# Mean and scale rows of tiles 6, 7 and 8: fetched through DRAM instead of turned on the tensor engine

## The chip, the cores and the metric

The kernel runs on one core of one Trainium2 chip. The metric is the device time of one execution in microseconds (us); the profile of one such execution stands beside it. The engines are named as in the profile: PE (matmul; PEld is its weight load), DVE (vector), ACT (scalar), POOL (GpSimd) and SP, which here only issues DMAs, in the order of its queue.

## The reference

One block over x of 2048 rows by 576: a layer norm, a linear-attention branch with 32 heads of 18, and a gated feed-forward branch of width 4608, multiplied and added to x.

```python
xn = layernorm(x)                       # per row: (x - mean) / sqrt(var + 1e-5)
q, k, v = split_heads(xn @ wqkv)
phi = lambda t: where(t > 0, t + 1, exp(t)) + 1e-6
kv, z = sum over s of phi(k) v,  sum over s of phi(k)
o = phi(q) kv / (phi(q) z + 1e-6);   s = o @ wo
g = silu((gelu(xn @ w_gate) * (xn @ w_up)) @ w_down)
out = x + s * g
```

## The kernel before

The 2048 rows are 16 tiles of 128 rows (`n` or `t` 0 to 15), four to a block `tb` (0 to 3, `TT` = 4); two blocks make one half `s`. Everything here concerns the first 170 us, where x is normalized, k and v are projected and kv is summed. The order of each engine is the order in which the code records its instructions (`act` L123, `vec` L126, `mm` L129, `pool` L132, `dma` L135 pin them), so an instruction that waits holds up all that stands behind it on its engine.

Tiles 0 to 3 are normalized with rows on the partitions and then transposed on PE (`xt`). For tiles 4 to 15 x is loaded a second time already transposed (`xt[n]`, the part `D:` of a tile `x_n`; two tiles per load), so the mean and the scale are needed along the free axis:

- `spread(n0, n)` takes the statistics of n tiles on DVE (`bn`, `mv`) and their logarithm and exponent on ACT (`st`); `scales(n0)` makes the scale from them in three small DVE operations. Each gives one number per partition.
- `turn(n)` gets the rows on PE: it broadcasts mean and scale of one tile to 128 columns and transposes them into one PSUM bank, `ms` (two transposes, L233).
- The other way, in `scales` and `sort_rows`: one DVE copy puts the mean beside the scale, SP stores 128 x 4 numbers to DRAM (`md`) and reads them back broadcast over all partitions (`mx`, 128 x 512, 256 KB; it waits until `md` has landed), and ACT sorts them into four rows (`mr`, 128 x 512). Before the change this is done for pairs 8, 10, 12 and 14, and used for tiles 9 to 15; tile 8 is still turned.
- `place(n)` for n of 4 and more is `normalize`: DVE subtracts the mean (`x<-x,ms` or `x<-x,mr`, 128 x 768), multiplies with the scale twice (`xf_B`, 128 x 384), ACT makes the high words (`xo_B`) and DVE the low words. PE reads them for k, v and, once a block is complete, q.

`kv_tile(t)` is the pass over one tile: the products `kv_0`, then (even t) the pair sums `kv_a` of the two tiles before, the rows of tile t+1 (`sort_rows` if a pair stands ready in `mixed`, then `turn`), the post-processing of k on DVE, `kv_1`, `place(t+1)`, post-processing (`e_k`, `pk`, `va`), `kv_2`, and what the list `end` holds. `x_next(n)` takes the statistics of a pair when n is even. (For n of 4 and more an odd n leaves it without work.)

After tile 7 come the q products of blocks 0 and 1: `q_store(tb, gi)` is one product `q_gi` on PE, relu and exp on ACT (`e_q`), one DVE operation and one POOL addition (`ph`), and a store. The dictionary `behind` hangs other work after single ones: the statistics of pair 8 after (0, 0), `scales(8)` after (0, 1), the rows of tile 8 after (0, 3), `place(8)` after (1, 0), the statistics of pair 10 after (1, 1). Then tile 8 starts. The buffers `mx`, `mr` and `ph` share six slots (`gl_tile`).

Of the kernel before, what the change touches and what calls it, by code (L numbers as in the profile page):

```python
# [26 lines left out]
TT = TBN // P  # L27
# [64 lines left out]
def block_kernel(ctx, tc, x, xe, xt, wq_d, wkv_d, wo, wgu_d, wd_d, out):  # L92
# [6 lines left out]
    def bank(name):  # L99
        return ps.tile([P, 512], F32, tag="one", bufs=6, name=name)  # L100
# [13 lines left out]
    def gl_tile(shape, name, dt=F32):  # L114
        return sb.tile(shape, dt, tag="gl", bufs=6, name=name)
# [6 lines left out]
    def act(*args, **kw):  # L122
        pin(nc.scalar.activation(*args, **kw))  # L123

    def vec(op, *args, **kw):
        pin(getattr(nc.vector, op)(*args, **kw))  # L126
# [7 lines left out]
    def dma(out, in_, eng=None):  # L134
        tc.keep_in_program_order((eng or nc.sync).dma_start(out=out, in_=in_))  # L135
# [18 lines left out]
    def load_x(n, k):  # L154

        if n % 2 == 0:
            shape = [P, 2, 2, 3 * P] if n < TT else [P, 2, D + 6 * P]
            xstat[n // 2] = big(14 + n // 2 % 2, shape, F32, f"x_{n}")
        t = xstat[n // 2][:, n % 2 : n % 2 + k]
        if n == 0:  # L160
            for j in range(2):
                dma(out=t[:, 0, j], in_=xe[0:P, j], eng=(nc.sync, nc.scalar)[j])
        elif n < TT:
            dma(out=t, in_=xe[n * P : (n + k) * P].rearrange("(t p) j d -> p t j d", p=P))
        else:
            dma(out=t[:, :, 0:D], in_=x[n * P : (n + k) * P].rearrange("(t p) d -> p t d", p=P))
            dma(out=t[:, :, D:], in_=xt[n : n + k].rearrange("t p m -> p t m"))

    def spread(n0, n):

        bn = sb.tile([P, TT, 12], F32, tag="bn", bufs=2, name=f"bn_{n0}")
        mv = sb.tile([P, 2 * TT, 2], F32, tag="mv", bufs=4, name=f"mv_{n0}")
        for t in range(n):
            xs = xstat[(n0 + t) // 2][:, (n0 + t) % 2]
            for j in range(2):
                src = xs[:, j, 0:HALF] if n0 < TT else xs[:, j * HALF : (j + 1) * HALF]
                vec("bn_stats", out=bn[:, t, 6 * j : 6 * j + 6], in_=src)
            vec("bn_aggr", out=mv[:, t, :], in_=bn[:, t, :])
        st = sb.tile([P, 6, TT], F32, tag="st", bufs=4, name=f"st_{n0}")
        act(st[:, 0, 0:n], mv[:, 0:n, 1], AF.Ln, bias=eps_t)  # L180
        act(st[:, 2, 0:n], st[:, 0, 0:n], AF.Exp, scale=-0.5)
        vec("tensor_scalar", st[:, 1, 0:n], mv[:, 0:n, 1], LN_EPS, None, op0=ALU.add)
        mom[n0] = n, mv, st

    def scales(n0):

        n, mv, st = mom.pop(n0)
        v, r, c = (st[:, i, 0:n] for i in range(1, 4))
        if n == 1:
            vec("tensor_scalar", c, r, r, -0.5, op0=ALU.mult, op1=ALU.mult)  # L190
            vec("tensor_scalar", c, c, v, 1.5, op0=ALU.mult, op1=ALU.add)
            vec("tensor_scalar", c, c, r, None, op0=ALU.mult)
        else:
            vec("scalar_tensor_tensor", c, r, -0.5, r, op0=ALU.mult, op1=ALU.mult)
            vec("tensor_mul", c, c, v)
            vec("scalar_tensor_tensor", c, c, 1.5, r, op0=ALU.add, op1=ALU.mult)
        for t in range(n):
            scale_of[n0 + t] = mv[:, t, 0:1], c[:, t : t + 1]
        if n0 >= 2 * TT:
            vec("tensor_copy", st[:, 3, 2:4], mv[:, 0:2, 0])  # L200
            d = dr.tile([P, 4], F32, name=f"md_{n0}")
            mixed[n0] = g = gl_tile([P, P, 4], f"mx_{n0}")
            dma(out=d, in_=st[:, 3, :])
            dma(
                out=g.rearrange("p t c -> p (t c)"),
                in_=d.rearrange("t c -> (t c)")[None, :].to_broadcast([P, 4 * P]),
            )

    def sort_rows(n0):

        g = gl_tile([P, 4, P], f"mr_{n0}")
        act(g, mixed.pop(n0).rearrange("p t c -> p c t"), AF.Copy)
        for t in range(2):
            if n0 + t > 2 * TT:
                rows_of[n0 + t] = [g[:, None, i + t] for i in (2, 0)]

    def center(n):

        if n >= TT:
            return  # L220
        xs = xstat[n // 2][:, n % 2]
        m, r = scale_of.pop(n)
        vec("tensor_scalar", xs, xs, m, r, op0=ALU.subtract, op1=ALU.mult)

    def turn(n, new=bank):

        xs = xstat[n // 2][:, n % 2]
        if n in rows_of:
            return
        if n >= TT:  # L230
            xts[n] = t = bank(f"ms_{n}")
            for i, v in enumerate(scale_of.pop(n)):
                pin(nc.tensor.transpose(  # L233
                    t[:, i * P : (i + 1) * P], v.to_broadcast([P, P]), ident
                ))
            return
        tiles = [new(f"xt_{n}_{j}") for j in range(2)]
        xts[n] = [t[:, 0 : 3 * P].rearrange("p (k t) -> p k t", k=3) for t in tiles]
        for j in range(2):
            for k in range(3):  # L240
                pin(nc.tensor.transpose(xts[n][j][:, k, :], xs[:, j, k * P : (k + 1) * P], ident))  # L241
# [59 lines left out]
    mom, scale_of, xts, rows_of, mixed = {}, {}, {}, {}, {}  # L301
# [12 lines left out]
    def difference(s, i):  # L314
        f = xf[s]
        nm, a, b, o = SUMS[i]
        vec("tensor_sub", f[o], f[a], f[b])
        f[nm] = f[o]

    def keep(s, nm, o):  # L320
        d = dr.tile([P, 5, TBN], F32, name=f"kept_{s}_{nm}")
        dma(out=d, in_=o.bitcast(F32))
        store[s, nm] = d
# [59 lines left out]
    def load_q(j):  # L383
        raws["q", j] = big(12, [P, 2, 3, Q2], F32, f"rq_{j}")
        dma(out=raws["q", j], in_=wq_d[:, j].rearrange("c p k f -> p c k f"))

    def prep_q(c, j):
        raw, main = raws["q", j][:, c], wq[j]
        cs, r = slice(c * Q2, (c + 1) * Q2), slice(2 * KR, 3 * KR)
        act(main[:, 0:3, cs], raw, AF.Copy)  # L390
        for o, src, hi in (
            (main[:, 3, cs], raw[:, 0, :], main[:, 0, cs]),
            (wq_l[:, j, cs], raw[:, 1, :], main[:, 1, cs]),
            (main[r, 2, cs], raw[r, 2, :], main[r, 2, cs]),
        ):
            pool("tensor_sub", o, src, hi.bitcast(F32))
# [117 lines left out]
    def kv_tile(t, late_=(), end=()):  # L514

        ahead = t % (2 * TT) != 2 * TT - 1
        x_mm(t, 0)
        if t % 2 == 0:
            kv_pair(t)
        n0 = (t + 1) // 2 * 2  # L520
        if n0 in mixed:
            sort_rows(n0)
        if ahead:
            turn(t + 1)
        k_post(t, 0)
        x_mm(t, 1)
        if ahead:
            place(t + 1)
            save(t + 1)
        k_post(t, 1)  # L530
        v_post(t, 1)
        run(list(late_))
        x_mm(t, 2)
        run(list(end))
        v_post(t, 2)
# [32 lines left out]
    def q_store(tb, gi):  # L568
        if tb not in ph_d:
            ph_d[tb] = dr.tile([P, NHG, TBN], F32, name=f"phd_{tb}")  # L570
        o = gl_tile([P, TBN], f"ph_{tb}_{gi}")
        q_mm(tb, gi, o)
        dma(out=ph_d[tb][:, gi, :], in_=o)
# [807 lines left out]
    spread(0, 1)  # L1381
    _, mv0, st0 = mom[0]
    scales(0)
    center(0)
    for v in (mv0[:, 0, 0:1], st0[:, 2, 0:1], st0[:, 3, 0:1]):
# [8 lines left out]
    place(0, (1,), (0,))  # L1394
    spread(1, 1)
    scales(1)
    center(1)
    place(0, (1,), (1,))
# [56 lines left out]
    def x_next(n):  # L1455

        if n % 2 == 0:
            spread(n, 2)
            scales(n)
        center(n)  # L1460
# [17 lines left out]
    load_q(0)  # L1478
    for n in range(3, 2 * TT):
        ends = []  # L1480
        if n < 2 * TT - 2:
            ends.append(lambda n=n: x_next(n + 2))
        if n >= TT:
            j, c = divmod(n - TT, 2)
            prep_q(c, j)
            if n == TT + 1:
                load_q(1)
        if n == 2 * TT - 1:
            ends += [lambda i=i: difference(0, i) for i in range(3)]
        kv_tile(n, end=ends)  # L1490
        if n in (4, 6):
            load_x(n + 4, 2)
        if n == TT:
            for nm in BS[0]:
                keep(0, nm, xo[0][nm])
        if n == TT:
            q_store(0, 4)
        if n == TT + 3:
            keep(0, "B22", xo[0]["B22"])

    N0 = 2 * TT
# [18 lines left out]
    def form_apart(nm):  # L1520
# [17 lines left out]
        ],  # L1538
        (0, 1): [lambda: scales(N0), lambda: form("T1")],
        (0, 2): [lambda: form_apart("T3")],  # L1540
        (0, 3): [lambda: turn(N0)],
        (1, 0): [lambda: place(N0)],
        (1, 1): [lambda: form("T2"), lambda: spread(N0 + 2, 2), lambda: scales(N0 + 2)],
    }
# [4 lines left out]
    for n in range(N0, 2 * N0):  # L1549
        ends = []  # L1550
# [73 lines left out]
    for q in range(NQ):  # L1624
        g = q // 2
# [66 lines left out]
```

## Time and profile before

| | us |
|---|---|
| median of 3 runs | 1455.42 |
| lowest and highest | 1454.8, 1455.93 |
| the profiled execution, device time | 1454.71 |
| its span, first to last instruction | 1453.0 |
| PE busy | 1446.4 |
| DVE, ACT, POOL busy | 1146.2, 565.5, 579.3 |

The profile shows one execution. A row of a timeline has the start, the time spent, the engine, the line, the operation, its tiles (output <- inputs), their shapes and the count; in square brackets the idle time of the engine before it and what ended it. Rows that follow each other are merged, so a row with x2 holds two instructions. Times are counted from the start of the span.

### The profile page before, as it was taken

Reading aid. Unit: us, or ns where it says so; the run is one execution under the profiler, and the core shown is the slowest. Engines: PE = TensorE matmul, PEld = TensorE weight load, DVE = VectorE, ACT = ScalarE, POOL = GpSimd, SP = SyncE. Lnnn points to the kernel's source line nnn. Section 1 sums busy time; section 2 is a strip of 40 time slices with the busy share of each in tenths; the row PEclk is TensorE's granted clock in tenths of the full one; section 3 lists DMA queues with packets and bytes.
Section 4 is the critical chain, followed back from the end, with each engine's and each line's share of the span. In section 5 each row is a group of like instructions: output and inputs, shape, how many; then the busy total and the mean of one; then the engine's idle time right before and its main releaser. Section 6 shows DMA issues by size and latency. Waiting matters only on the chain.

```text
span 1453.0 us, 22169 instructions
## 1 busy us (share of the span) xinstructions
PE 1446.4 (100%) x8272; PEld 1289.0 (89%) x8272; DVE 1146.2 (79%) x1609; ACT 565.5 (39%) x918; POOL 579.3 (40%) x520
## 2 busy tenths in 40 slices
PE   9999999999999999999999999999999999999998
PEld 8989989988888888888888888888889999999998
DVE  7688667376787887887777878777878978989898
ACT  6444365333232233322332232332236555545454
POOL 3342440225756567565575755667632000000000
PEclk9999999999999999999999999999999999999999
DMA  5554115621532315224242343324289887767886
GB/s 224 187 205 152 45 42 201 225 93 51 174 102 95 130 54 186 87 95 145 77 149 87 102 145 109 113 84 136 115 277 343 265 262 254 246 183 238 277 290 224
DMA packets 119237, 235.04 MB, mean 162 GB/s; under 512 B 11658, under 2 KB 45322, under 8 KB 117210
## 3 DMA queue, kind: packets, MB, share of 16 engines
q1 hardware_dynamic: 116330, 221.37, 45.2%
q0 software_dynamic: 2656, 12.06, 2.2%
q8 instruction: 65, 1.06, 0.3%
q14 instruction: 42, 0.34, 0.1%
q10 hardware_dynamic: 144, 0.20, 0.0%
HBM read 150.96 MB, written 82.58 MB: 161 GB/s over the span
## 4 chain that ended last, share of the span: by engine, by line
PE 97%; DVE 1%; ACT 1%; issue 0%; POOL 0%; DVEq 0%; ACTq 0%; POOLq 0%
PE bd L129 25%; PE al L887 16%; PE de L887 16%; PE ga L887 16%; PE kv L129 8%; PE be L887 8%; PE s L129 4%; PE q L129 3%; PE kv_a L129 1%; PE idle L129 0%; PE d L129 0%; PE kw L129 0%; PE b L129 0%; ACT e_q L123 0%; PE xt L241 0%
## 5 line engine op out<-in xcount | busy, mean ns | idle before, releaser
L132 POOL TENSOR_TENSOR sm<-raw 128x384 f32<-128x384 f32 x72 | 75.0, 1042 | 144.3 <-DMA raw<-in_wgu_dram 113.3
L129 PE MATMUL kv<-wkv,xo_B 128*128 128x412 f32 (+2 forms) x662 | 125.0, 347 | 0.3 <-ACT xo_B L123 0.3
L129 PEld LDWEIGHTS kv<-wkv,xo_B 128*128 128x128 f32 x662 | 120.3, 188 | 1.7 <-ACT xo_B L123 0.8
L126 DVE TENSOR_TENSOR wa<-sm,wa 128x768 fp32r<-128x768 f32 x72 | 92.2, 1281 | 36.1 <-ACT wa L123 35.2
L129 PE MATMUL bd<-w_head,hi 128*128 128x288 f32 x516 | 118.0, 294 | 0.0
L126 DVE TENSOR_TENSOR wb<-raw,wb 128x256 fp32r<-128x256 f32 (+1 forms) x108 | 101.2, 937 | 7.4 <-ACT wb L123 5.8
L126 DVE TENSOR_TENSOR wa<-raw,wa 128x256 fp32r<-128x256 f32 x72 | 65.6, 911 | 50.7 <-ACT wa L123 47.5
L123 ACT ACTIVATE hi<-raw_h 128x1024 fp32r<-128x1024 f32 x59 | 62.5, 1059 | 93.0 <-PE bd L129 56.5
L129 PE MATMUL bd<-w_end,hi 128*128 128x288 f32 x448 | 89.8, 294 | 0.0
L123 ACT ACTIVATE spot_h<-spot_h 128x512 f32<-128x512 f32 x49 | 30.8, 633 | 149.4 <-DVE spot_h L126 149.4
L129 PEld LDWEIGHTS bd<-w_head,hi 128*128 128x128 f32 x516 | 87.0, 188 | 0.1
L126 DVE TENSOR_TENSOR raw_h<-raw_h,hi 128x1024 fp32r<-128x1024 f32 x59 | 71.7, 1220 | 19.1 <-ACT hi L123 18.9
L129 PE MATMUL bd<-w_end,raw_h 128*128 128x288 f32 x264 | 77.9, 295 | 0.0
L123 ACT ACTIVATE wa<-sm 128x1152 fp32r<-128x1152 f32 x36 | 41.8, 1161 | 91.1 <-PE de L887 91.1
L123 ACT ACTIVATE u<-al 128x512 f32<-128x512 f32 x72 | 41.0, 592 | 89.9 <-PE al L887 68.1
L129 PEld LDWEIGHTS bd<-w_end,hi 128*128 128x128 f32 x448 | 71.8, 188 | 0.0
L129 PE MATMUL bd<-beside,raw_h 128*128 128x288 f32 x240 | 70.8, 295 | 0.0
L132 POOL TENSOR_TENSOR spot_h<-spot_h,spot_h 128x512 f32<-128x512 f32 x45 | 62.5, 1396 | 2.9 <-DVE spot_h L126 2.4
L887 PE MATMUL al<-xo_B,wa 128*128 128x512 f32 x252 | 63.0, 389 | 0.0
L887 PE MATMUL al<-xo_B,wb 128*128 128x512 f32 x252 | 63.0, 389 | 0.0
L887 PE MATMUL be<-xo_T,wa 128*128 128x512 f32 x252 | 63.0, 389 | 0.0
L887 PE MATMUL be<-xr_T,wa 128*128 128x512 f32 x252 | 63.0, 389 | 0.0
(278 smaller groups left out, 4036.0 us busy)
## 6 DMA issues: line engine op xcount, KB each, us to landing
raw_h<-hs SPq DMA_DIRECT2D x176, 256.0 KB
raw<-in_wgu_dram SPq DMA_DIRECT2D x36, 768.0 KB
hs<-spot_h SPq DMA_DIRECT2D x90, 256.0 KB
hs<-spot_g SPq DMA_DIRECT2D x80, 256.0 KB
b<-in_wd_dram SPq DMA_DIRECT2D x42, 432.0 KB
hs<-spot_m SPq DMA_DIRECT2D x38, 256.0 KB
raw_g<-hs SPq DMA_DIRECT2D x22, 256.0 KB
raw_a<-hs SPq DMA_DIRECT2D x20, 256.0 KB
```

The source lines that it names most:

```text
L123: pin(nc.scalar.activation(*args, **kw))
L126: pin(getattr(nc.vector, op)(*args, **kw))
L129: pin(nc.tensor.matmul(*args, **kw))
L132: pin(getattr(nc.gpsimd, op)(*args, **kw))
L887: nc.tensor.matmul(o, w[0:rows, wi, :], xop[0:rows, xi, :], start=(start and n == 0), stop=(n == len(PASSES) - 1), skip_group_check=True,)
```

## The change

Pairs from tile 6 on (instead of tile 8 on) go through DRAM, and both tiles of a pair take their rows from there, so tiles 6, 7 and 8 are no longer turned. The statistics and scales of tiles 6 and 7 are taken at the end of tile 3 (they were at the end of tile 4). The sorting of pair 8 stands where the turn of tile 8 stood, after q product (0, 3); it was in `kv_tile(8)`. The sorting of pair 6 comes in `kv_tile(5)`.

```diff
@@ scales
-        if n0 >= 2 * TT:
+        if n0 >= TT + 2:
             vec("tensor_copy", st[:, 3, 2:4], mv[:, 0:2, 0])
             d = dr.tile([P, 4], F32, name=f"md_{n0}")
@@ sort_rows
         for t in range(2):
-            if n0 + t > 2 * TT:
-                rows_of[n0 + t] = [g[:, None, i + t] for i in (2, 0)]
+            rows_of[n0 + t] = [g[:, None, i + t] for i in (2, 0)]
@@ block_kernel
     for n in range(3, 2 * TT):
         ends = []
-        if n < 2 * TT - 2:
-            ends.append(lambda n=n: x_next(n + 2))
+        if n == 3:
+            ends.append(lambda: x_next(6))
@@ behind
-        (0, 3): [lambda: turn(N0)],
+        (0, 3): [lambda: sort_rows(N0)],
```

How it moves instructions, at the three places of which the prediction speaks. First ACT between the q products (0, 3) and (1, 0), where `e_q_3` belongs to (0, 3), `e_q_0` to (1, 0) and the `xo_B` to tile 8. Before:

```order
L123 ACTIVATE e_q_3_1095<-q_3_1080 128x512
L123 ACTIVATE e_q_3_1095<-e_q_3_1095 128x512
L123 ACTIVATE e_q_0_1120<-q_0_1105 128x512
L123 ACTIVATE e_q_0_1120<-e_q_0_1120 128x512
L123 ACTIVATE xo_B_1127<-xf_B_1128 128x3x128
L123 ACTIVATE xo_B_1130<-xf_B_1131 128x3x128
```

And with the change:

```order
L123 ACTIVATE e_q_3_1096<-q_3_1081 128x512
L123 ACTIVATE e_q_3_1096<-e_q_3_1096 128x512
L123 ACTIVATE mr_1102<-mx_1038 128x512
L123 ACTIVATE e_q_0_1120<-q_0_1105 128x512
L123 ACTIVATE e_q_0_1120<-e_q_0_1120 128x512
L123 ACTIVATE xo_B_1127<-xf_B_1128 128x3x128
L123 ACTIVATE xo_B_1130<-xf_B_1131 128x3x128
```

The sorting of pair 8 now stands ahead of `e_q_0`; it had stood one q block later, behind the last `e_q_3`.

Next DVE at the end of tile 3; `kv_1` there is tile 3's, the `e_k` and `pk` behind belong to tile 4's `kv_0`. With the change:

```order
L126 TENSOR_SCALAR pk_511<-kv_1_515 128x160
L126 BN_STATS bn_565<-x_448 128x6 x2
L126 BN_AGGR mv_566<-bn_565 128x2
L126 BN_STATS bn_565<-x_448 128x6 x2
L126 BN_AGGR mv_566<-bn_565 128x2
L126 TENSOR_SCALAR st_573<-mv_566 128x2
L126 SCALAR_TENSOR_TENSOR st_573<-st_573 128x2
L126 TENSOR_TENSOR st_573<-st_573 128x2
L126 SCALAR_TENSOR_TENSOR st_573<-st_573 128x2
L126 COPY st_573<-mv_566 128x2
L126 TENSOR_SCALAR e_k_631<-kv_0_592 128x416
```

Before, `e_k` followed `pk` there directly, and the statistics stood one tile later without the copy.

Last SP's queue in tile 4, with the loads of tiles 8 and 9 (`x_684`):

```order
L135 DMA rq_491<-in_wq_dram 128x2x768
L135 DMA md_581<-st_573 128x4
L135 DMA mx_582<-md_581 128x512
L135 DMA x_684<-in_x_dram 128x2x576
L135 DMA x_684<-in_xt_dram 128x2x768
```

The store `md` and the read `mx` of pair 6 now stand ahead of that load. On PE six transposes are gone; nothing else changes its order.

## The prediction

> **What bounds the kernel now.** I read the page first, then PE's waits, then the timeline of the first 150 us, where everything stands that the change touches.
>
> ```profile
> PE 1446.4 (100%) x8272; PEld 1289.0 (89%) x8272; DVE 1146.2 (79%) x1609; ACT 565.5 (39%) x918; POOL 579.3 (40%) x520
> PE 97%; DVE 1%; ACT 1%; issue 0%; POOL 0%; DVEq 0%; ACTq 0%; POOLq 0%
> PEld kv L129 <- ACT xo_B L123: 0.8, 2, 0.6
> 114.61 10.30 PEld L129 LDWEIGHTS kv<-wkv,xo_B 128*128 128x128 f32 x56 [0.62 <-ACT xo_B L123]
> ```
>
> PE is busy all along (1446.4 of 1453.0 us) and makes 97% of the chain that ended last. So a PE instruction less is time won, as long as PE's operands come in time; work on DVE, ACT or SP costs nothing until PE waits for it. In the whole kernel PE's weight load waited for normalized tiles 0.8 us, and 0.62 us of that is one wait, at 114.61: PE had come to `kv_0` of tile 9 and ACT had not yet made that tile's `xo_B`. There, and there alone among the tiles that the change touches, the chain through DVE and ACT is already later than PE. What delays that chain is paid in full.
>
> I followed it back from the wait. It is a row of instructions in which each begins when another ends:
>
> ```profile
> 94.37 0.64 ACT L123 ACTIVATE e_q<-e_q 128x512 f32<-128x512 f32 x1
> 97.15 0.60 ACT L123 ACTIVATE e_q<-q 128x512 f32<-128x512 f32 x1 [2.14 <-PE q L129]
> 97.78 0.69 DVE L126 TENSOR_SCALAR ph<-q 128x512 f32<-128x512 f32 x1 [0.20 <-ACT e_q L123]
> 98.50 0.95 DVE L126 TENSOR_TENSOR x<-x,ms 128x768 f32<-128x768 f32 x1
> 99.49 1.02 DVE L126 TENSOR_TENSOR xf_B<-x,ms 128x384 f32<-128x384 f32 x2
> 100.08 0.99 ACT L123 ACTIVATE xo_B<-xf_B 128x384 fp32r<-128x384 f32 x2 [1.67 <-DVE xf_B L126]
> 100.97 0.58 ACT L123 ACTIVATE e_q<-q 128x512 f32<-128x512 f32 x1
> 102.12 1.48 ACT L123 ACTIVATE xo_T<-xf_B 128x1536 fp32r<-128x1536 f32 x1
> 103.63 2.44 DVE L126 TENSOR_TENSOR xo_T<-xf_B,xo_T 128x1024 fp32r<-128x1024 f32 x2 [0.76 <-ACT xo_T L123]
> 106.10 0.82 DVE L126 BATCH_NORM_STATS2 bn<-x 128x6 f32<-128x288 f32 x2
> 108.12 0.29 ACT L123 ACTIVATE st<-mv,eps_t 128x2 f32<-128x2 f32 x1 [4.52 <-DVE mv L126]
> 110.33 0.69 DVE L126 TENSOR_SCALAR ph<-q 128x512 f32<-128x512 f32 x1 [0.42 <-ACT e_q L123]
> 112.02 1.38 DVE L126 TENSOR_TENSOR x<-x,mr 128x768 f32<-128x768 f32 x1
> 114.03 1.00 ACT L123 ACTIVATE xo_B<-xf_B 128x384 fp32r<-128x384 f32 x2 [2.04 <-DVE xf_B L126]
> ```
>
> From the relu of q product (1, 0) at 97.15 over the normalization of tile 8 (98.50 to 100.08), the relu of (1, 1), the form T2 on ACT and DVE (102.12, 103.63), the statistics of pair 10 (106.10, 108.12) and the last `ph` (110.33) to tile 9 (112.02, 114.03) no step has room: the idle times in brackets are waits for the step before. So a microsecond lost at 97 is a microsecond lost at 114.61.
>
> **What is won on PE.** Three pairs of transposes go. Two of them lie ahead of the chain above:
>
> ```profile
> 56.24 0.13 PEld L233 LDWEIGHTS ms<-ident,mv 128*128 128x128 f32 x1
> 56.54 7.63 PEld L129 LDWEIGHTS kv<-wkv,xo_B 128*128 128x128 f32 x42
> 65.83 0.13 PEld L233 LDWEIGHTS ms<-ident,mv 128*128 128x128 f32 x1
> 65.99 12.72 PEld L129 LDWEIGHTS kv<-wkv,xo_B 128*128 128x128 f32 x70
> ```
>
> From the first load of a pair to the next product's load it is 0.30 us for tile 6 and 0.16 for tile 7: PE, and all that follows it, runs 0.46 us earlier from there. The third pair (tile 8) is worth about 0.3 as well, but PE then only comes earlier to the wait at 114.61: that part is lost.
>
> **What moves onto the chain.** The third turn is replaced by the sorting of pair 8. It stands on ACT right behind the exp at 94.37 and ahead of the relu at 97.15, and it needs the rows from DRAM:
>
> ```profile
> 91.70 0.38 SPq L135 DMA_DIRECT2D md<-st  x1
> 94.91 0.32 SPq L135 DMA_DIRECT2D mx<-md  x1
> 95.34 0.37 SPq L135 DMA_DIRECT2D kept_T<-xo_T  x1
> 145.98 0.34 SPq L135 DMA_DIRECT2D mx<-md  x1
> 148.50:149.00 0.50, 0.50 (x4) 0.50 (x4) 0.28 (x2) 0.42 (x1) 0.00 (x0) 1.00 0.19 57
> 149.00:149.50 0.50, 0.50 (x5) 0.49 (x4) 0.00 (x0) 0.50 (x3) 0.10 (x1) 1.00 0.00 0
> 117.86 1.15 ACT L123 ACTIVATE mr<-mx 128x512 f32<-128x512 f32 x1
> ```
>
> In before nobody waits for pair 8's rows (they are sorted in tile 8), so no row says when they land; I bound it. Their read is issued at 94.91. Pair 14's read, issued at 145.98 with nothing beside it, still moves 57 GB/s in the half microsecond up to 149.00 and nothing after: 3.1 us from issue to the last byte. Pair 8's has the store `kept_T` (1280 KB) behind it in the queue from 95.34, so I take 3.4 us: landed at 98.3, in before's time. With the 0.46 us that PE is ahead it is 97.85.
>
> ACT is free at about 94.5 and would wait 3.3 us with `e_q` of (1, 0) behind it. Then the sorting takes 1.15 (row 117.86, the same shape). ACT's next instruction starts about 0.1 before the end of the one ahead (100.08 + 0.99 is 101.07, and the next starts at 100.97), so `e_q` starts at 97.85 + 0.04 + 1.05 = 98.94 instead of 97.15: **+1.8 us**, the PE lead already taken off. Waiting for it are DVE's `ph`, the whole of tile 8's normalization, and POOL. Bounds: 98.0 (3.1 us) gives +1.5; 4.0 us gives +2.4.
>
> **What changes within tile 8's normalization.** Its operand comes from SBUF (`mr`) instead of PSUM (`ms`).
>
> ```profile
> L126 DVE TENSOR_TENSOR x<-x,mr x7: 948/958/1383, 112.0 to 161.5; 128x768 f32<-128x768 f32 x7
> 110.04 2.55 POOL L132 TENSOR_TENSOR ph<-ph,e_q 128x512 f32<-128x512 f32 x2 [5.75 <-DVE ph L126]
> 97.75 2.54 POOL L132 TENSOR_TENSOR ph<-ph,e_q 128x512 f32<-128x512 f32 x2 [1.44 <-ACT e_q L123]
> ```
>
> Alone both forms take the same (0.96 and 0.95). But the one `x<-x,mr` that meets a POOL addition, at 112.02, takes 1.38: POOL's pair ends at 112.59, and it ends 0.81 after that. `x<-x,ms` at 98.50 ran beside POOL's pair of 97.75 and took its 0.95. So reading `mr` beside POOL costs what is left of POOL's addition less 0.15 (0.57 left, 0.43 lost). With the change POOL's addition for (1, 0), 1.27 long, becomes ready when `ph` ends, and so does `x<-x,mr`: both want to start within 0.1 us of each other. If POOL is first, the subtraction waits for all of it, 1.27 - 0.15 = 1.1; if the subtraction is first, POOL comes between it and `xf_B`, which then waits the same. **+1.1 us**; bounds 0 (as beside `ms`) and 1.3.
>
> [...]
>
> **The other edits.** Statistics of tiles 6 and 7 at the end of tile 3: is x there?
>
> ```profile
> 38.00:40.00 2.00, 2.00 (x14) 1.94 (x13) 1.18 (x3) 0.00 (x0) 0.00 (x0) 1.00 0.10 33
> 33.98 0.31 DVE L126 TENSOR_SCALAR pk<-kv 128x160 f32<-128x160 f32 x1
> 36.79 0.48 ACT L123 ACTIVATE va<-kv 128x252 f32<-128x252 f32 x2
> 43.73 0.32 DVE L126 TENSOR_SCALAR pk<-kv 128x160 f32<-128x160 f32 x1
> 46.68 1.25 PEld L129 LDWEIGHTS kv_a<-pk,va 128*64 128x64 f32 x40 [0.27 <-issue]
> ```
>
> Yes: the loads issued in tile 2 are through by 40 (DMA share 0.10 from 38 to 40), and DVE comes to it at 44. But ACT's logarithm and exponent now stand ahead of tile 3's last `va`. At the end of tile 2, where the same stands today, `va` starts 2.81 after DVE's `pk` (33.98, 36.79) and takes 0.48. Put behind 43.73 that is 47.02, while the 40 loads of `kv_a`, 1.25 us from 46.68 and the second half of a pair's first groups at 47.2, need it: room 0.15 us. I take 0.1 (bounds 0 and 0.5). DVE's `e_k` of tile 4 starts half a microsecond later and waits for `kv_a` behind it anyway. Pair 6's `md` and `mx` are in SP's queue at about 47.5, ahead of the load of tiles 8 and 9, which today waits for its buffer until about 50.7 (tile 5's last `xf_B`); its statistics come forty microseconds later, so a delay is covered. Sorting pair 6 in tile 5 (1.15 on ACT) falls where logarithm and exponent were: cost nothing. Tiles 6 and 7 now also read `mr` beside POOL's `wq`; each has over a microsecond before PE needs it: nothing. Removing the sorting from tile 8 wins nothing, since DVE at 112.02 came there straight from `pk`.
>
> **The sum**, against the profiled execution: 1454.71 + 1.8 + 1.1 + 0.1 = 1457.7 us. The median of the runs lies 0.7 us above that execution, so for the median 1455.42 + 3.0 = **1458.4 us**.
>
> **The rivals.**
> - *The rows come early.* If `md` lands as fast as pair 10's, the sorting hardly holds ACT:
>
> ```profile
> 109.34 0.32 SPq L135 DMA_DIRECT2D md<-st  x1
> 110.82 0.32 SPq L135 DMA_DIRECT2D mx<-md  x1
> ```
>
> There `mx` follows 1.5 us after `md`; for pair 8 it was 3.2. With 1.5 + 3.1 pair 8's rows land at 96.3 - 0.46 = 95.8, ACT is through at 96.9, and the relu starts no later than 97.15. It decides at a landing before about 96.5. Then the wait is gone and at most the collision with POOL stays: 1455.4 to 1456.4, not slower by what counts. Against it: nothing that stands ahead of pair 8's `md` in the queue changes. [...] Chance 0.08.
> - *The wait, but no collision* (POOL is past, or shares): +1.8 + 0.1, 1457.3. Chance 0.18.
> - *PE waits earlier, too.* The late `va` holds PE at 47.2 (0.5), or tile 6 or 7 comes late through POOL (up to 1): this adds to the forecast, 1459.5. Nothing in the waits of before shows it. Chance 0.09.
> - *The change gives what it says:* no wait anywhere, three pairs gone: -0.8 us, 1454.6. For that the wait at 114.61 would have to vanish, which nothing in it does. Chance 0.02.
> - The forecast, wait and collision: 0.61. The remaining 0.02 is for what I don't see.
>
> **How the numbers follow.** 0.2% is 2.9 us, about what a measurement of this kernel can tell from no change; that puts the limit at 1458.3, within the forecast's own spread (1457.6 to 1459.2). Its open sizes lean upward (a landing up to 4.0 us, POOL's part up to 1.3, `va`), so I give three quarters of it, 0.46, to the slower side and 0.15 to the same. Slower: 0.46 + 0.09 = 0.55. Same: 0.15 + 0.18 + 0.08 + 0.02 = 0.43. Faster: the 0.02 left. The range runs from 1455.9 (between the early rows and the wait without collision) to 1459.9.
>
> **What would show it.** Right: ACT idle for some 3 us ahead of a `mr<-mx` near 98, put down to DMA `mx`; `e_q` of (1, 0) near 99; `xf_B` or `x<-x,mr` of tile 8 about a microsecond longer than 0.55 or 0.95; PE's wait at tile 9 grown from 0.62 to nearly 4 us and ended by ACT `xo_B`; the rest of the kernel shifted by one amount. Wrong: that wait unchanged, an ACT that finds the rows there, a new PE wait before 60 us, or a difference that arises after 170 us.

## The result, and the profile after

The changed kernel takes 1457.97 us (median of 20 runs, 1456.54 to 1460.06) against 1455.51 for the kernel before on the same chip (20 runs, 1454.67 to 1457.07): 1.0018 times as long, interval 1.0011 to 1.0025. The median is 2.5 us longer, a little short of the 0.2% that was named as the limit for slower. Forecast were 1458.4 (+3.0) and a range of 1455.9 to 1459.9; the runs lie in it but for two.

First the page of the changed kernel (busy times, shares of the chain), then PE's waits, as engine, line, releaser: us in total, times, longest.

```profile
PE 1446.6 (99%) x8266; PEld 1288.8 (89%) x8266; DVE 1153.6 (79%) x1610; ACT 566.4 (39%) x919; POOL 581.5 (40%) x520
PE 94%; DVE 3%; DMA 1%; ACT 1%; issue 1%; POOL 0%; SPq 0%; ACTq 0%; DVEq 0%; POOLq 0%
PEld kv L129 <- ACT xo_B L123: 3.4, 2, 3.2
PEld bd L129 <- DVE raw_h L126: 1.0, 3, 0.3
PE kv L129 <- ACT xo_B L123: 2.9, 1, 2.9
```

PE's own work is what it was (1446.6 us; 1446.4 before), the span is 1455.8 instead of 1453.0. PE now stands still once, for 2.9 us, and the one wait of its weight load that had been 0.62 is 3.2. The chain that ended last no longer runs through PE alone: DVE has 3% of it instead of 1%. The timelines of the changed kernel, of SP, ACT, DVE, POOL and PEld in this order, show the whole step:

```profile
91.43 0.38 SPq L135 DMA_DIRECT2D md<-st  x1
93.17 0.32 SPq L135 DMA_DIRECT2D mx<-md  x1
94.11 0.63 ACT L123 ACTIVATE e_q<-e_q 128x512 f32<-128x512 f32 x1
97.26 1.13 ACT L123 ACTIVATE mr<-mx 128x512 f32<-128x512 f32 x1 [2.52 <-DMA mx<-md]
98.29 0.58 ACT L123 ACTIVATE e_q<-q 128x512 f32<-128x512 f32 x1
98.90 0.69 DVE L126 TENSOR_SCALAR ph<-q 128x512 f32<-128x512 f32 x1 [1.60 <-ACT e_q L123]
99.62 0.96 DVE L126 TENSOR_TENSOR x<-x,mr 128x768 f32<-128x768 f32 x1
100.62 2.00 DVE L126 TENSOR_TENSOR xf_B<-x,mr 128x384 f32<-128x384 f32 x2
97.47 1.30 POOL L132 TENSOR_TENSOR ph<-ph,e_q 128x512 f32<-128x512 f32 x1 [1.44 <-DVE ph L126]
99.73 2.00 POOL L132 TENSOR_TENSOR ph<-ph,e_q 128x512 f32<-128x512 f32 x1 [0.96 <-DVE ph L126]
116.12 0.99 ACT L123 ACTIVATE xo_B<-xf_B 128x384 fp32r<-128x384 f32 x2 [3.06 <-DVE xf_B L126]
116.69 3.48 PEld L129 LDWEIGHTS kv<-wkv,xo_B 128*128 128x128 f32 x19 [3.21 <-ACT xo_B L123]
```

ACT is free at 94.74 and stands for 2.52 us until the rows have landed. The relu `e_q` of (1, 0) starts at 98.29 instead of 97.15: 1.14 late. The two `xf_B` of tile 8 take 2.00 instead of 1.02: another 0.98. From there the chain runs in the same steps as before and 2.1 us later, and PE takes up tile 9 at 116.69 instead of 114.61: 2.08 late. 1.14 + 0.98 is 2.12. PE's instructions from there to 1230 us keep that distance within 0.1 us. In this execution 0.7 us more come in the last stage, where PE's products `bd` wait for DVE's `raw_h` three times 0.3 us instead of once, as this line of before has it:

```profile
PEld bd L129 <- DVE raw_h L126: 0.3, 1, 0.3
```

### The profile page after: what moved, and what is told of

The parts are those of the page before. It is cut to its first block, busy times and chain, and to the rows that moved or that the text cites. A ratio compares the mean times of both kernels' runs of the same rounds, so it can differ in the third digit from the quotient of the medians.

```text
span 1455.8 us, 22159 instructions
## 1 busy us (share of the span) xinstructions
PE 1446.6 (99%) x8266; PEld 1288.8 (89%) x8266; DVE 1153.6 (79%) x1610; ACT 566.4 (39%) x919; POOL 581.5 (40%) x520
## 4 chain that ended last, share of the span: by engine, by line
PE 94%; DVE 3%; DMA 1%; ACT 1%; issue 1%; POOL 0%; SPq 0%; ACTq 0%; DVEq 0%; POOLq 0%
PE bd L129 23%; PE al L886 16%; PE ga L886 16%; PE de L886 16%; PE be L886 8%; PE kv L129 7%; PE s L129 4%; PE q L129 2%; DMA raw_h<-hs 1%; PE kv_a L129 1%; DVE raw_h L126 0%; ACT e_q L123 0%; PE idle L129 0%; PE d L129 0%; PE kw L129 0%
## 5 line engine op out<-in xcount | busy, mean ns | idle before, releaser
L886 PE MATMUL al<-xr_B,wa 128*128 128x512 f32 x252 | 63.0, 389 | 0.0
```

The costliest lines, as they stand in the source:

```text
L886: nc.tensor.matmul(o, w[0:rows, wi, :], xop[0:rows, xi, :], start=(start and n == 0), stop=(n == len(PASSES) - 1), skip_group_check=True,)
```

## The experiments

My theory: the wait for `mx` ahead of `e_q`, and the collision of DVE with POOL in tile 8, are the whole loss, and the other edits gain a little. The rivals: the early statistics or pair 6 cost something; one of the two terms makes all of it; the loss arises elsewhere. Starts are compared with the profile before. PE's first 20 us come out up to 0.6 us longer from one execution to the next, with all that follows shifted alike; distances at tile 9 are given without that shift, which is read at 18 to 50 us.

**e1: pair 6 through DRAM, tile 8 turned as before.** Against the changed kernel:

```diff
-            rows_of[n0 + t] = [g[:, None, i + t] for i in (2, 0)]
+            if n0 + t != 2 * TT:
+                rows_of[n0 + t] = [g[:, None, i + t] for i in (2, 0)]
-        (0, 3): [lambda: sort_rows(N0)],
+        (0, 3): [lambda: turn(N0)],
```

> Tiles 6 and 7 through DRAM with their statistics at the end of tile 3, as changed; tile 8 turned on PE after (0, 3) and pair 8 sorted in tile 8, as before. My theory (all of the loss is pair 8's sorting ahead of the relu of (1, 0), with its wait and the collision with POOL): PE comes 0.3 to 0.5 us earlier from tile 7 on, no row of ACT waits for mx, PE's wait at tile 9 is 0.6 us as before, and the kernel is 0.4 us faster than before (1455.1). Rival (pair 6's path costs: statistics at tile 3, POOL beside tiles 6 and 7, or the changed buffers): it stays 1 us or more slower than before.

Measured: 1454.69 us against 1455.72 before, ratio 0.9993 (0.9984 to 1.0002). PEld of e1 at tile 9:

```profile
114.58 4.61 PEld L129 LDWEIGHTS kv<-wkv,xo_B 128*128 128x128 f32 x25 [0.62 <-ACT xo_B L123]
```

The wait is the old one. So statistics at tile 3, pair 6's DMAs and tiles 6 and 7 by `mr` cost nothing; the loss is in pair 8.

**e2: the wait alone.** Pair 8 is sorted after (0, 3), but tile 8 still uses the turned rows:

```diff
+            if n0 + t != 2 * TT:
+                rows_of[n0 + t] = [g[:, None, i + t] for i in (2, 0)]
-        (0, 3): [lambda: sort_rows(N0)],
+        (0, 3): [lambda: sort_rows(N0), lambda: turn(N0)],
```

> As changed, but tile 8 takes its rows from the turn on PE, put right behind pair 8's sorting, which keeps its place ahead of the relu of (1, 0). So ACT's wait for mx is kept and the two SBUF inputs of tile 8's normalization go. My theory (wait and collision each cost by themselves): ACT still waits 2.5 us, the relu starts 1.1 us later than before, xf_B of tile 8 takes its usual 0.55 each, PE resumes at tile 9 about 1.1 us later than before (2.1 in the changed kernel): +1.1 us, 1456.6. Rival (the collision costs nothing by itself, since the wait would have held the chain as long anyway): as slow as the changed kernel, +2.1 or more.

**e3: the collision alone.** The statistics of pair 8 come at the end of tile 6, so that the rows are there early:

```diff
-        if n0 in mixed:
+        if n0 in mixed and t != 7:
-        if n == 3:
-            ends.append(lambda: x_next(6))
+        if n in (3, 6):
+            ends.append(lambda n=n: x_next(6 if n == 3 else 8))
-            lambda: kv_pair(N0), lambda: q_store(1, 4), lambda: spread(N0, 2),
+            lambda: kv_pair(N0), lambda: q_store(1, 4),
-        (0, 1): [lambda: scales(N0), lambda: form("T1")],
+        (0, 1): [lambda: form("T1")],
```

> As changed, but the statistics, the scale and the two DMAs of pair 8 stand at the end of tile 6 instead of after (0, 0) and (0, 1); the sorting stays after (0, 3). So the rows are there and the wait goes, the collision stays. My theory: no ACT wait ahead of mr; the relu of (1, 0) at 96.7; xf_B of tile 8 still takes 2.0 for two beside POOL's addition; PE resumes at tile 9 0.4 to 0.6 us later than before: +0.5 us, 1456.0. By the rival that the wait alone is the loss: -0.5 us, 1455.0. By the rival that the sorting's 1.15 us on ACT is what counts: +1 or more.

Measured: e2 1456.63 (1.0007, 0.9998 to 1.0016), e3 1455.55 (1.0, 0.9991 to 1.0009). ACT, DVE and PEld, three lines of e2:

```profile
97.79 1.12 ACT L123 ACTIVATE mr<-mx 128x512 f32<-128x512 f32 x1 [2.91 <-DMA mx<-md]
101.14 1.02 DVE L126 TENSOR_TENSOR xf_B<-x,ms 128x384 f32<-128x384 f32 x2
116.26 2.72 PEld L129 LDWEIGHTS kv<-wkv,xo_B 128*128 128x128 f32 x12 [2.40 <-ACT xo_B L123]
```

and four of e3:

```profile
94.88 1.11 ACT L123 ACTIVATE mr<-mx 128x512 f32<-128x512 f32 x1
96.89 0.60 ACT L123 ACTIVATE e_q<-q 128x512 f32<-128x512 f32 x1 [0.90 <-PE q L129]
99.23 2.00 DVE L126 TENSOR_TENSOR xf_B<-x,mr 128x384 f32<-128x384 f32 x2
115.34 3.69 PEld L129 LDWEIGHTS kv<-wkv,xo_B 128*128 128x128 f32 x20 [1.61 <-ACT xo_B L123]
```

Each kernel shows one term and not the other. In e2 ACT waits 2.91 us and `xf_B` takes its 1.02; in e3 ACT waits for nothing but PE's q, and `xf_B` takes 2.00. At tile 9 PE is 1.52 late in e2, 0.71 in e3, 2.1 in the changed kernel with both, and 0.25 early in e1 with neither. Against e1, which has neither, the collision is worth 0.71 + 0.25 = 0.96, the same as the lengthened `xf_B`. The wait is worth 1.52 + 0.25 = 1.77 in e2. In the changed kernel it is the rest, 2.1 + 0.25 - 0.96 = 1.4 (the relu is 1.14 late against before, and the lead of 0.25 is lost with it); its rows landed 0.4 us earlier than those of e2 (0.5 as the starts stand, less e2's shift of 0.13). So the two terms add up in the profiles. The medians tell less: e3's, 0.2 us below before, lies between the theory's +0.5 and the -0.5 of the rival by which the wait alone is the loss. What decides between the two is the `xf_B` row and PE's start at tile 9.

**e4: e3 with pair 10's statistics moved from (1, 1) to (0, 1)**, to shorten the chain behind tile 8.

```diff
-        (0, 1): [lambda: form("T1")],
+        (0, 1): [lambda: spread(N0 + 2, 2), lambda: form("T1")],
-        (1, 1): [lambda: form("T2"), lambda: spread(N0 + 2, 2), lambda: scales(N0 + 2)],
+        (1, 1): [lambda: form("T2"), lambda: scales(N0 + 2)],
```

> As e3_early_rows, and the statistics of pair 10 taken from (1, 1) to (0, 1), where pair 8's scale stood; pair 10's scale and DMAs stay after (1, 1). It takes 2 us of DVE and ACT's logarithm and exponent out of the chain to tile 9. My theory (PE's time is set only by that chain at tile 9): PE's wait at tile 9 is gone, all three pairs of transposes (0.7 us) and the 0.6 us wait of before are won: -1.3 us, 1454.2, faster than both. Rival (the collision or another wait takes its place): between -0.3 and +1.

Measured: 1456.02 (1.0001, 0.9992 to 1.001): missed. DVE and PEld of e4:

```profile
98.55 1.29 DVE L126 TENSOR_SCALAR ph<-q 128x512 f32<-128x512 f32 x2
99.87 1.65 DVE L126 TENSOR_TENSOR x<-x,mr 128x768 f32<-128x768 f32 x1
115.06 4.07 PEld L129 LDWEIGHTS kv<-wkv,xo_B 128*128 128x128 f32 x22 [0.97 <-ACT xo_B L123]
126.75 0.32 PEld L129 LDWEIGHTS kv_a<-pk,va 128*64 128x64 f32 x8 [0.57 <-POOL va L132]
127.56 0.50 PEld L129 LDWEIGHTS kv_a<-pk,va 128*64 128x64 f32 x16 [0.49 <-ACT va L123]
```

The statistics make DVE late at the head of the chain: tile 8's subtraction starts at 99.87 instead of 98.24 in e3, and it meets POOL as well (1.65 instead of 0.96). That returns a part of what their absence behind it saves, and PE is still 0.04 late at tile 9 (0.71 in e3). But what is won there is lost again in tile 10's pass, where the pair sums `kv_a` now wait for `va` (the last two rows): PE stands still for 0.76 us, which it does not do there in e3.

**e5: no wait, no collision, shorter chain.** Against e1: pair 8's statistics at the end of tile 6, pair 10's at (0, 0), and pair 8 sorted after (0, 3) from rows that are long there; tile 8 is turned.

```diff
-        if n0 in mixed:
+        if n0 in mixed and t != 7:
-        if n == 3:
-            ends.append(lambda: x_next(6))
+        if n in (3, 6):
+            ends.append(lambda n=n: x_next(6 if n == 3 else 8))
-            lambda: kv_pair(N0), lambda: q_store(1, 4), lambda: spread(N0, 2),
+            lambda: kv_pair(N0), lambda: q_store(1, 4), lambda: spread(N0 + 2, 2),
-        (0, 1): [lambda: scales(N0), lambda: form("T1")],
+        (0, 1): [lambda: form("T1")],
-        (0, 3): [lambda: turn(N0)],
+        (0, 3): [lambda: sort_rows(N0), lambda: turn(N0)],
-        (1, 1): [lambda: form("T2"), lambda: spread(N0 + 2, 2), lambda: scales(N0 + 2)],
+        (1, 1): [lambda: form("T2"), lambda: scales(N0 + 2)],
```

> As e1_pair6_only (tiles 6 and 7 through DRAM, tile 8 turned on PE), but pair 8's statistics, scale and DMAs stand at the end of tile 6, pair 10's statistics after (0, 0) where pair 8's were, and pair 8's sorting, whose rows are then long there, after (0, 3). It takes 2 us of DVE and a round over ACT out of the chain from the relu of (1, 0) to tile 9 without putting work on DVE in its place. My theory (the chain through DVE and ACT sets PE's wait at tile 9): the wait of 0.6 us goes, 1.6 us faster than before, 0.6 faster than e1_pair6_only (1454.1). Rival (DVE is full there and gives the time back elsewhere, as in e4_rows_and_stats10): no better than e1_pair6_only.

Measured: 1454.43 against 1455.66 before (0.9996, 0.9987 to 1.0005; 1453.85 to 1458.81): the lowest median of the kernels run, not told apart from before by the interval. PEld of e5 passes tile 9 without a stop:

```profile
106.19 18.13 PEld L129 LDWEIGHTS kv<-wkv,xo_B 128*128 128x128 f32 x98
```

**e6: the change, with pair 8 sorted behind (1, 0), just ahead of `place(8)`,** so that `e_q` does not wait:

```diff
-        (0, 3): [lambda: sort_rows(N0)],
-        (1, 0): [lambda: place(N0)],
+        (1, 0): [lambda: sort_rows(N0), lambda: place(N0)],
```

> As changed, with pair 8's sorting one step later on ACT, behind relu and exp of (1, 0) and right ahead of tile 8's normalization. ACT then waits for the rows without holding the relu. My theory: the relu of (1, 0) at 96.7 as PE allows, the sorting from 97.9 to 99.0, DVE's subtraction behind it beside or after POOL's addition; PE resumes at tile 9 0.7 to 1.3 us later than before, half of the changed kernel's loss: +1.0 us. Rival (only the landing of the rows counts, wherever the sorting stands): +2 or more.

Measured: 1457.72 (1.0013, 1.0005 to 1.0022). ACT, DVE and PEld of e6:

```profile
97.02 0.60 ACT L123 ACTIVATE e_q<-q 128x512 f32<-128x512 f32 x1 [1.91 <-PE q L129]
99.33 1.87 DVE L126 TENSOR_TENSOR x<-x,mr 128x768 f32<-128x768 f32 x1 [0.99 <-ACT mr L123]
116.35 2.67 PEld L129 LDWEIGHTS kv<-wkv,xo_B 128*128 128x128 f32 x11 [2.49 <-ACT xo_B L123]
```

`e_q` is on time; the subtraction waits 0.99 for `mr` and then takes 1.87 instead of 0.95 beside POOL. PE is 1.39 late at tile 9, instead of 2.1.

**e7: the kernel before with nothing but tile 8's rows through DRAM** (pair 6 as before):

```diff
-            if n0 + t > 2 * TT:
+            if n0 + t >= 2 * TT:
-        (0, 3): [lambda: turn(N0)],
+        (0, 3): [lambda: sort_rows(N0)],
```

> The kernel before with one edit: pair 8's rows serve tile 8 too, sorted after (0, 3) in place of its turn; tiles 6 and 7 are turned as before, their statistics at the end of tile 4. My theory: all of the loss is here, and without the 0.5 us that pair 6 wins: PE's wait at tile 9 grows by 2.5 us, +2.5 to +3.0 us (1458.3). Rival (pair 6's part takes part in the loss): +1.5 or less.

Measured: 1460.41 against 1455.66 (1.0032, 1.0021 to 1.0043), more than expected. SP, ACT and PEld of e7, and three stretches with PE's busy time first and the granted clock third from the end:

```profile
92.44 0.38 SPq L135 DMA_DIRECT2D md<-st  x1
95.52 0.32 SPq L135 DMA_DIRECT2D mx<-md  x1
99.08 1.12 ACT L123 ACTIVATE mr<-mx 128x512 f32<-128x512 f32 x1 [3.34 <-DMA mx<-md]
118.48 0.50 PEld L129 LDWEIGHTS kv<-wkv,xo_B 128*128 128x128 f32 x2 [3.99 <-ACT xo_B L123]
116.00:118.00 2.00, 0.00 (x0) 0.00 (x0) 1.97 (x3) 0.09 (x1) 0.47 (x1) 0.99 0.63 91
118.00:120.00 2.00, 1.51 (x4) 1.46 (x5) 1.76 (x5) 0.90 (x2) 0.00 (x0) 0.50 1.06 330
120.00:122.00 2.00, 2.00 (x9) 1.93 (x9) 0.56 (x2) 1.57 (x6) 0.81 (x1) 0.66 0.87 299
```

Two things are new here. `md` has landed 3.1 us after its issue; in the changed kernel it was 1.7. And behind the wait PE runs at half its clock: in the trace's record of the clock from 117.96 to 121.38, 3.41 us, and the three stretches, granted 0.99, 0.50 and 0.66, make the same 3.4 us. PE is 3.23 late at tile 9, and 1.3 more at 121.4; of the 1.3, 1.0 is left at 170 us.

**e8, e9, e10, e11: does the half clock come from PE's idle gap?** Products of 128 x 128 that nothing uses are added ahead of `kv_0` of tile 9, in a bank of their own; the work is added to the reference's. e8 is e7 with 24 calls (48 matmuls), e10 with 16; e9 is the changed kernel with 16; e11 is e7 again, on e10's chip.

```diff
+        if t == 9:
+            fill = bank("fill")
+            for _ in range(24):
+                mm(fill[:, 0:P], ident, ident, start=True, stop=True)
```

> As e7 (tile 8's rows through DRAM, sorted after (0, 3)), with 24 products of 128 x 128 on PE, results unused, ahead of kv_0 of tile 9, where PE stood idle for about 4 us. They add work that the reference does not have. Theory (PE's idle gap at tile 9 is what halves the granted clock for 3.41 us right behind it): a PE that is busy in most of the gap shows no row with half the clock between 115 and 125 us, tile 9 begins as late as in e7 (PE about +3.2 at tile 9), but the products behind it run at full clock: median 1458.6 to 1459.2, some 1.3 to 1.7 less than e7's 1460.4. Rival (the whole loss is the late chain, the low clock is a side effect that costs nothing or comes from elsewhere): 1460.4 or more, or the half clock is still there.

> The changed kernel with 16 products of 128 x 128 on PE, results unused, ahead of kv_0 of tile 9, where PE stood idle for 2.9 us. Theory (some executions of the changed kernel lose another 1.3 to 1.7 us to half the clock behind that gap): no run near 1460, all between 1456.5 and 1458.9, median 1457.3 to 1457.9. Rival (the spread of the changed kernel comes from elsewhere): as the changed kernel, 1458.0 median and one run in five from 1459.6 to 1460.1.

> e8 with 16 instead of 24 added products, so that they end before tile 9's xo_B is there (a pair of its matmuls took 0.115 us in e8, so 3.7 us from 114.05: to about 117.7, against 118.3 for xo_B). Theory: the products now cost nothing, the late chain costs what it costs in e7 (PE +3.2 at tile 9), and the 1.3 us of the half clock behind it are gone: no granted clock below 1.0 near 120, median 1.0 to 1.5 us below e7's on the same chip. Rival (the half clock costs nothing that counts): the same median as e7 within 0.4.

> The same kernel as e7, on the chip of e10, for the comparison. Expected as there: 0.5 for 3.4 us behind tile 9's wait, 1460.4, between 1459.7 and 1461.

Measured: e8 1460.83 and e9 1458.3, against 1455.05 before on their chip (1.0038 and 1.0019); e10 1459.34 and e11 1459.57, against 1455.15 on theirs (1.0028, 1.0018 to 1.0037; 1.003, 1.0019 to 1.0041). The stretch behind the wait, of e10 and then of e11, and PEld of both:

```profile
118.00:120.00 2.00, 1.97 (x11) 1.85 (x11) 1.76 (x6) 0.55 (x2) 0.00 (x0) 1.00 1.03 291
114.20 3.71 PEld L129 LDWEIGHTS fill<-ident 128*128 128x128 f32 x32
118.13 2.00 PEld L129 LDWEIGHTS kv<-wkv,xo_B 128*128 128x128 f32 x11 [0.22 <-ACT xo_B L123]
```

```profile
118.00:120.00 2.00, 2.00 (x7) 1.90 (x8) 1.76 (x6) 0.48 (x2) 0.00 (x0) 0.50 0.95 284
117.82 2.45 PEld L129 LDWEIGHTS kv<-wkv,xo_B 128*128 128x128 f32 x8 [4.08 <-ACT xo_B L123]
PEld ga L887 <- DVE u L126: 0.9, 1, 0.9
```

(The 0.115 us of the expectation for e10 is that of one matmul, 48 in 5.50 us in e8, not of a pair; e10's 32 took 3.71.) Filling the gap takes the half clock away, and that part is shown: e10 is granted 1.00 in each stretch from 112 to 124 us, e11 on the same chip 0.50 and 0.65 from 118 to 122. e8 has 1.00 from 110 to 124 as well, where e7 had 0.50 and 0.66. So has e9, but the changed kernel had 1.00 there without the products. In e10 PE keeps its distance at tile 9 to the end of the kernel; in e11 1.3 us come on top behind tile 9. But the medians that were forecast for e8, e9 and e10 were all missed. The medians of e10 and e11 lie only 0.2 us apart, not 1.0 to 1.5; there the rival's number held, so that a gain in the runs is not shown. e8 cannot judge it, since its products ran 1.2 us past the point where `xo_B` was ready. e9 was no faster than the changed kernel, 3.2 us above before on its chip, and its runs go up to 1459.52; its products ran past that point too, by 0.25 us. The runs of e10, all with a mean clock of 0.999 or 1.0, still spread from 1457.8 to 1460.7. Single waits of about 1 us in later stages are of the size of that spread: the one of `ga` (a product of a later stage) for DVE's `u` stands near 495 us in the profiles of e2, e5, e7, e8 and e11 and not in the others. What sets them off stays open.

## Why the prediction was right, point by point

- *PE bounds, and a microsecond lost at 97 is one lost at 114.61:* right. 2.12 us lost at 97 to 102 became 2.08 at tile 9.
- *The wait of ACT for `mx`, +1.8:* right in place and mechanism, too large. It was 1.14. The step that failed is the landing: I read pair 8's `md` of before as it stood (3.2 us) because nothing ahead of it in SP's queue changes. In the five kernels whose profile has both pair 6 through DRAM and pair 8's statistics in their old place (the changed one, e1, e2, e6, e9) `mx` follows `md` by 1.74 us, in those with pair 6 turned (before, e7, e8, e10, e11) by 2.9 to 3.3. `mx` itself took longer than assumed (4.0 instead of 3.4), so the rows came at 97.2 instead of 97.85. Why the small store lands sooner wasn't found out. Pair 6 cannot be the only thing that sets it: in before, with pair 6 turned, `mx` follows `md` by 1.48 us for pairs 10 and 12 and by 2.31 for pair 14. In e7, with the landing as assumed, ACT waited 3.34 us; 3.3 was forecast.
- *The collision with POOL, +1.1:* right, 0.98; e2 and e3 take it apart from the wait. The subtraction kept its 0.96 while POOL's addition, alone 1.30, took 2.00 beside it, and then `xf_B`, 1.02 for two beside `ms`, took 2.00 beside that: the subtraction lost nothing, POOL 0.70 and `xf_B` 0.98. How the two engines come to hold each other up was not shown. The operation that paid was `xf_B`, the second of the two that were named, since the subtraction was first by 0.1 us; in e6 it was the subtraction.
- *`kv_a` and `va`, +0.1:* nothing. Of ACT and PEld in the changed kernel:

```profile
46.54 0.49 ACT L123 ACTIVATE va<-kv 128x252 f32<-128x252 f32 x2
46.67 1.25 PEld L129 LDWEIGHTS kv_a<-pk,va 128*64 128x64 f32 x40 [0.27 <-issue]
```

  `va` came at 46.54, half a microsecond ahead of the estimate, and `kv_a` started as before (46.68). Tiles 6 and 7 cost nothing either (e1).
- *The lead from the removed transposes, 0.46, is lost at the wait:* lost, yes. In size it was not 0.46 but 0.3 us from tiles 6 and 7, with another 0.2 from tile 8: the distances between weight loads, from which it was read, are not the time that PE itself gains.
- *The sum:* 1.8 + 1.1 + 0.1 = 3.0 stands against 2.1 at tile 9 and 2.8 at the end of the profiled execution. That the total fits so well is partly luck: the wait was 0.7 too big, and 0.7 came from `bd` in the last stage, which the sum did not have. "A difference that arises after 170 us" was among the signs of an error, and this is one, though a small one. The median, +2.5, lies between the two.

## What to carry to other kernels

Before an operation is put on an in-order engine, look at what stands behind it: here a sorting that waited 2.52 us for its rows held a relu that did not need them (1.14 late), and with it a chain that had no slack for the next 17 us. Look too at what a helper operand's reader meets when the operand moves from PSUM to SBUF: here two `xf_B` took 1.02 beside POOL's addition with `ms` (e2), 2.00 beside it with `mr` (e3), and 1.03 with `mr` alone (tile 9 in before). If a step is to go through DRAM, start it one stage earlier: in e3 and e5 ACT's wait for the rows was gone, while moving the sorting (e6) left the subtraction a wait of 0.99.

## What the runs showed of the hardware

The granted clock of PE fell to a half for about 3.4 us around the end of some of PE's gaps at tile 9, and not the length of the gap alone decided. The gap is what PE's busy time leaves of the stretches from 112 to 120 us, the clock that of the stretches from there on:

| kernel | PE idle, us | granted clock |
|---|---|---|
| before, e1 | 0.30 | 1.00 |
| e4 | 0.65 | 1.00 |
| e3 | 1.29 | 1.00 |
| e2 | 2.07 | 0.94, 0.50, 0.70 (116 to 122) |
| changed kernel | 2.88 | 1.00 |
| e7 | 3.68 | 0.99, 0.50, 0.66 (116 to 122) |
| e11 | 3.76 | 1.00, 0.50, 0.65 (116 to 122) |

The changed kernel's gap of 2.88 us keeps its clock, and e2's of 2.07 loses it:

```profile
114.00:116.00 2.00, 0.00 (x0) 0.00 (x0) 1.97 (x3) 0.00 (x0) 0.68 (x1) 1.00 0.68 125
116.00:118.00 2.00, 1.31 (x7) 1.30 (x8) 1.78 (x6) 0.99 (x2) 0.00 (x0) 1.00 0.92 299
```

```profile
116.00:118.00 2.00, 1.74 (x9) 1.71 (x10) 1.75 (x6) 0.68 (x2) 0.00 (x0) 0.94 0.95 268
118.00:120.00 2.00, 2.00 (x7) 1.92 (x6) 0.34 (x2) 1.80 (x6) 1.04 (x1) 0.50 0.95 332
```

(The first fence is the changed kernel's, the second that of e2.) Summed over their stretches, e2 runs at half clock for 3.44 us, e7 and e11 for 3.40. Why the gap of 2.88 us kept the clock was not shown. The slow stretch costs PE work: from 118 to 122 us the rows hold 25 of its products in the changed kernel, 16 in e2 and in e11, and 13 in e7, where PE resumed at 118.48. At 25 in 4 us that is about 1.4 us in each, an estimate; PE's starts gave 1.3 in e7 and e11. That some runs of the changed kernel had it too is only argued: five of its 20 show a mean clock of 0.998 or less, and their median is 1459.9, that of the others 1457.8. A mean of 0.998, as rounded, takes at least 4.4 us at half clock (an estimate: twice 0.0015 of 1458 us); the changed kernel's profile, with a mean of 0.999, has 2.2, all at its end.
